# A fused attention, expert and slot-expert kernel on one core: a written-out sequence of all operations instead of priorities

## The chip, the core and the metric

The kernel runs on one NeuronCore of a Trainium2 chip. Its engines work in parallel, each through its own list of instructions, strictly in the order of the list: TensorE (PE, matrix products into the eight PSUM banks), VectorE (DVE), ScalarE (ACT), GpSimd (POOL) and SyncE (SP), which here issues all DMA transfers. They wait for each other by semaphores. The metric is the device time of one execution in microseconds (us); lower is better.

## What is computed

Three layers, on 4 x 576 = 2304 tokens of 512 features, all in float32:

```python
# 1: attention, 8 heads of 64, each token sees itself and the 63 tokens before it
scores = (q @ k.T) / 8, masked;  attn = softmax(scores);  x = attn @ v
# 2: a dense layer with mish
h = x @ w_in                      # 512 -> 2048
g = h * tanh(softplus(h))
y = g @ w_out                     # 2048 -> 512
# 3: soft routing to 8 experts of 4 slots
logits = y @ phi                  # 2304 x 32
d = softmax over tokens;  slot_input = d.T @ y
slot_out[e] = relu(slot_input[e] @ w1[e]) @ w2[e]
c = softmax over slots;   out = c @ slot_out
```

## The kernel before

The tokens form 18 tiles t of 128. The layer-2 output y is never formed: w_out is folded into phi (`wpmm`, from w_out transposed, tiles `wt`), so that logits come from g directly, and the sum over tokens is kept as A = d.T @ g (`A`, `Aup`) and multiplied by w_out (`wo`) once, in the tail.

Per attention tile, by the names of the operations: `qk` (scores, PE), `max`, `neg` (DVE), `exp` (ACT, two halves h of four heads), `sum`, `rcp` (DVE), `nrm` (POOL or DVE), `atr` (transposes of a half, PE), `tre` (their copy out of PSUM), `pv` (PE), `x` (copy). `vg` measures the size of a v tile for scaling. Then, per tile t and quarter m of w_in: `xh`, `xl` (x in two float16 parts), `mm{t}_{m}a` and `mm{t}_{m}b` (half products of six 128x512 float16 matmuls, line 727; the first two tiles use float32 in quarters 0 and 1, line 724), `mi` (mish, ACT, line 733), `gh`, `gl` (g in two float16 parts, lines 747 to 754), `tr` (a DMA transpose of both, issued by SP, line 760; tile 17 is transposed by PE instead), `lg` (logits), and per block of two tiles the running softmax over tokens `lt`, `bm`, `bexp`, `et`, `eh`, `el`, `A`, `Aup`. The weights w_in (`wi`), w_out (`wo`) and its transpose (`wt`) are loaded as 64-bit words and decoded to float32 by `a` (ACT, line 385), `b` and `d` (DVE, lines 390, 394). `wh`, `wl` are w_in in two float16 parts.

The tail: `tat`, `tate`, `tsi`, `tsie`, `tso`, `tsoe` (slot inputs), `t1` (16 products with w1), `relu`, `tho`, `thT`, `t2` (32 products with w2, line 1085, by column pieces of `W2C`), and for each piece `se`, `sr`, `sv` (spread the slot outputs), `fo` (products with c, line 1125), `ob` (copy, line 1131) and `st` (store, line 1138). w1 and w2 come as 64 loads `w0` to `w63` of 512 KB; each takes one of 53 slabs of SBUF, as do all k, q, v, weight and work tiles, and frees it after its last use.

ACT holds one table of functions at a time: exp and the decode use one (`E`), mish another (`M`); an `ACT_TABLE_LOAD` stands at each change. Copies and sums work with either.

The order is made when the program is built. `Plan` collects some 1,430 operations, each with an engine, a guessed cost, a priority, the operations it depends on and the buffers it takes and frees. `emit` then plays them through: whenever an engine is free in this play, it takes the ready operation of the lowest priority number whose buffers are free. The priorities are formulas of the tile number plus some 400 fitted shifts (`SHIFT`). `reserve` holds back slabs from the `w` loads. While PE would wait before the first quarter-3 product (`mm0_3a`), and again between the last product of tile 17 and `t1_0`, `emit` puts in pad products (`fill`, line 295: 128x256, of zeros, their result unused). What the program then contains is only the order on each engine; the costs play no part on the chip.

## Time and profile before

| | |
|---|---|
| runs (median of 3) | 388.83 us (387.75 to 388.90) |
| profiled execution | 387.64 us |
| its span | 385.8 us |
| PE busy | 368.3 us (95%) |
| DVE busy | 271.6 us (70%) |
| ACT busy | 255.0 us (66%) |
| POOL busy | 35.1 us (9%) |
| read from and written to HBM | 79.48 and 4.72 MB |
| instructions | 10397 |

The span is the time from the first to the last recorded work of the profiled execution. Busy is the union of an engine's instructions; a pad product counts as busy. The ends of matmuls are modelled, and in a row of back-to-back products the starts tell the pace. Idle time of an engine that is followed by other work is put down to what released it.

### The profile page before, as it was taken

To read this page: it belongs to the slowest core of one execution; us is meant where nothing else is said; L and a number is where in the kernel's file an instruction comes from. 1 tells how busy PE (TensorE), PEld (TensorE's weight loads), DVE (VectorE), ACT (ScalarE), POOL (GpSimd) and SP (SyncE) were. 2 spreads that over 40 slices of the span, in tenths; PEclk is the share of its full clock that TensorE was granted. 3 is DMA by queue.
4 is the path that set the end of the run, shared out by engine and by line. 5 is a ranking of instruction groups with operands and counts; after the bars stand their busy time and mean duration, and the time that the engine had idled before them with its cause. 6 is when DMAs were issued, how large, how long until landed. Compare 5 with 4: busy or idle time off the path is not lost.

```text
span 385.8 us, 10397 instructions
## 1 busy us (share of the span) xinstructions
PE 368.3 (95%) x4188; PEld 213.2 (55%) x4188; DVE 271.6 (70%) x781; ACT 255.0 (66%) x507; POOL 35.1 (9%) x33
## 2 busy tenths in 40 slices
PE   8999999999999798999999999999999999999981
PEld 6775646566655354685545445444644567534771
DVE  1879897798999878999999983678336567410241
ACT  2889999999999879799348744775299246000121
POOL 0033002605516000000000000000000000000000
PEclk9999999999999999999999999999999999999996
DMA  7999991079878989889899998999684999999996
GB/s 278 409 409 407 395 410 73 1 220 287 322 164 233 358 195 210 314 285 303 234 241 210 253 185 158 292 258 189 127 313 115 188 245 372 379 382 408 363 322 143
DMA packets 102912, 102.70 MB, mean 266 GB/s; under 512 B 78544, under 2 KB 83536, under 8 KB 102864
## 3 DMA queue, kind: packets, MB, share of 16 engines
q1 hardware_dynamic: 102864, 102.04, 89.7%
q8 instruction: 33, 0.54, 0.6%
q14 instruction: 15, 0.12, 0.1%
HBM read 79.48 MB, written 4.72 MB: 218 GB/s over the span
## 4 chain that ended last, share of the span: by engine, by line
PE 70%; DMA 10%; ACT 8%; DVE 6%; issue 3%; SPq 1%; DVEq 0%; ACTq 0%
PE h L727 32%; PE pad L295 4%; PE s L441 4%; PE eo L1085 4%; PE eh L1053 4%; DMA v<-in_vL 3%; PE px L526 3%; ACT p L469 3%; PE pt L513 3%; PE A L922 3%; DMA wor<-in_w_out 2%; PE lg L845 2%; PE h L724 2%; PE fo L1125 2%; DMA cst<-in_cst 2%
## 5 line engine op out<-in xcount | busy, mean ns | idle before, releaser
L727 PE MATMUL h<-wh,xx 128*128 128x512 f16 x544 | 171.6, 379 | 0.7 <-ACT pts L518 0.7
L727 PEld LDWEIGHTS <-xx 128*128 128x128 f16 x816 | 77.0, 98 | 88.3 <-issue 4.8
L727 PE MATMUL h<-wl,xx 128*128 128x512 f16 x272 | 103.1, 379 | 0.0
L733 ACT ACTIVATE u<-h,sc 128x512 f32<-128x512 f32 x68 | 44.0, 689 | 29.3 <-PE h L727 27.4
L754 DVE SCALAR_TENSOR_TENSOR gg<-u,sc,gg 128x1024 f16<-128x1024 f32 (+1 forms) x38 | 47.1, 1245 | 0.4
L733 ACT ACT_TABLE_LOAD x28 | 35.9, 1283 | 2.6 <-DVE wo L390 1.8
L483 POOL TENSOR_TENSOR p<-p,st 128x512 f32<-128x512 f32 x24 | 29.1, 1234 | 82.2 <-DVE sc L357 25.1
L469 ACT ACTIVATE p<-p,st 128x128 f32<-128x128 f32 x112 | 35.4, 394 | 0.1
L751 DVE TENSOR_SCALAR gg<-u,sc 128x1024 f16<-128x1024 f32 (+1 forms) x34 | 24.8, 741 | 11.9 <-ACT u L733 5.3
L462 DVE CUSTOM_DVE_ANT_0 p<-s,cb 128x128 f32<-128x128 f32 x112 | 25.5, 283 | 2.5 <-PE s L441 2.4
L295 PE MATMUL pad<-wphi 128*64 128x256 f16 x170 | 25.4, 299 | 0.9 <-DVE wphi L307 0.9
L513 PE MATMUL pt<-cst,p 128*128 128x128 f32 x144 | 22.1, 278 | 2.1 <-DVE st L462 1.6
L518 ACT COPY pts<-pt 128x512 f32<-128x512 f32 x36 | 20.7, 582 | 4.5 <-PE pt L513 4.5
L526 PEld LDWEIGHTS px<-pts,v 128*64 128x64 f32 x576 | 18.4, 138 | 8.1 <-issue 3.1
L526 PE MATMUL px<-pts,v 128*64 128x64 f32 x576 | 20.7, 225 | 2.0 <-DMA v<-in_vL 2.0
L295 PEld LDWEIGHTS <-wphi 128*64 128x64 f16 x170 | 18.8, 120 | 4.7 <-issue 2.0
L475 DVE TENSOR_REDUCE st<-p 128x4 f32<-128x512 f32 x28 | 18.8, 673 | 3.2 <-ACT p L469 3.1
L385 ACT ACT_TABLE_LOAD x14 | 18.0, 1283 | 4.3 <-DVE wo L394 1.4
L513 PEld LDWEIGHTS pt<-cst,p 128*128 128x128 f32 x144 | 16.1, 140 | 7.0 <-issue 2.3
L441 PE MATMUL s<-k,q 64*64 64x128 f32 x576 | 19.6, 275 | 0.0
L441 PEld LDWEIGHTS s<-k,q 64*64 64x64 f32 x576 | 15.5, 133 | 4.6 <-issue 2.6
L1131 ACT COPY ob<-fo 128x512 f32<-128x512 f32 (+3 forms) x14 | 5.3, 440 | 19.3 <-PE fo L1125 19.3
(175 smaller groups left out, 523.7 us busy)
## 6 DMA issues: line engine op xcount, KB each, us to landing
w<-in_wL SPq DMA_DIRECT2D x64, 512.0 KB, 7.0
v<-in_vL SPq DMA_DIRECT2D x18, 512.0 KB, 6.9
wir<-in_w_in SPq DMA_DIRECT2D x16, 512.0 KB, 9.7
wtr<-in_w_outT SPq DMA_DIRECT2D x16, 512.0 KB, 6.6
wor<-in_w_out SPq DMA_DIRECT2D x16, 512.0 KB, 4.6
k<-in_kL SPq DMA_DIRECT2D x12, 512.0 KB, 7.3
q<-in_qL SPq DMA_DIRECT2D x9, 512.0 KB, 9.3
out<-ob SPq DMA_DIRECT2D x6, 512.0 KB, 4.9
```

The lines of the kernel that those rows point to most:

```text
L295: PE.matmul(pad, lhsT=hot, rhs=hot.unsqueeze(1).to_broadcast([128, 4, 64]), start=True, stop=True)
L441: PE.matmul(st_[t][h][64 * c:64 * c + 64, p], lhsT=qt[t // 2][r, t % 2, p, 64 * c:64 * c + 64], rhs=kt[g // 3][r, p, 64 * (g % 3):64 * (g ...
L462: DVE.tensor_tensor_reduce(out=pr[t][:, h, p], in0=st_[t][h][:, p], in1=cb[:, mask(t)], scale=-0.125, scalar=3e38, op0=ALU.add, op1=ALU.mi ...
L469: ACT.activation(pr[t][:, h, p], (st_[t][h] if t < P["MP"] else pr[t][:, h])[:, p], AF.Exp, scale=0.125 if t < P["MP"] else -1.0, bias=sta ...
L483: (POOL if P["ND"] <= t < P["NRM"] else DVE).tensor_tensor(pr[t][:, h], pr[t][:, h], r, ALU.mult)
L513: PE.transpose(q[:, p], pr[t][:, h, p], ident)
L518: ACT.copy(ptS[t][:, h], pt_[t, h])
L526: PE.matmul(x[64 * h:64 * h + 64, p, f], lhsT=vt[t][:, c, 64 * (2 * p + h):64 * (2 * p + h) + 64], rhs=ptS[t][:, h, p, f], start=True, sto ...
L727: PE.matmul(ph[t, m], lhsT=xh[t][:, l, kk], rhs=r[m][:, kk], start=(kk == 0 and i == 0), stop=(kk == 3 and i == 2))
L733: ACT.activation(ub[t, h][:, m % 2], ph[t, m], AF.Mish, scale=1.0 if (t, m) in P["F32"] else col(INVH + 4 * PART[t] + m))
L751: DVE.tensor_scalar(o, u, col(CP + PART[t]), None, ALU.mult)
L754: DVE.scalar_tensor_tensor(gg[t, h][:, 1, c:c + n], flat(ub[t, h], c, n), col(CP + PART[t]), gg[t, h][:, 0, c:c + n], ALU.mult, ALU.subtract,)
```

## The change

All operations, their dependencies and their buffers stay, apart from four things. First, `emit` no longer chooses: it goes through a list of 1,428 names, `ORDER`, and issues each operation on its engine in that order. The priorities, the shifts and `reserve` are gone. The costs remain only to set where pads stand and which free slab is taken. Second, the engine of single casts and copies can be chosen one by one (`ENG`, `pick`, `two_ways`), and whether the row sums of a half tile's `exp` are made by ACT as it goes or by DVE afterwards. Third, the first q slab is loaded in two halves (`q0`, `q0b`), and tiles 0 and 1 invert their row sums by halves. Fourth, `W2C` has the columns 256, 128, 128 instead of 256, 128, 64, 64.

```diff
-    22, 19, 13, 3, 1, 0, 18, 12, 7), WQ=408.421, WQ_SP=1.144, A0=-11.663, A1=10, AK=12, A2=15, LEAD=15.837,
...
-    WO=-9.123, WO_SP=1.355, NU=9, NGC=14, NSC=4, FAST=2, PET=17, SINGLE=16, RB=8, W2C=((0, 256), (256, 128),
-    (384, 64), (448, 64)), QUART=17, VGA=(1, 3), TP=15.286, BL=66.703, NRM=13, VP=(-27.15, -25.68, -0.06,
...
+    PB=(2, 4, 8), NU=9, NGC=14, NSC=4, NX=2, PET=17, QUART=17, SINGLE=16, RB=8, RH=2, MP=4, VGN=2, GRAM=2,
+    TOP=0.77, W2C=((0, 256), (256, 128), (384, 128)), F32=((0, 0), (1, 0), (0, 1), (1, 1)),
+    ENG=dict(sum='000000000000000011001100110011001100110011001100010000000100110011',
+    nrm='0000110011001100110000000100100000000100010011001100110011000000000001',
...
+ORDER = """
+hot room_q0 q0 cb k0 cst wild0 wild2 eye k1 qk0 wia0 q0b max0_0 wild1 max0_1 wia2 neg0_1 neg0_0 q1 wib0 exp0_0 wib2
...
+gl1_0 qk11 v9
+tre7_0 xl4 wta5 atr7_1 nrm8_1 wtld14 pv6 gh0_1 max11_0 mm4_0a exp9_1 max11_1 v8 invh2_0 wtb5 atr8_0 tre7_1 sum9_1
+atr8_1 tre8_0 wtd5 mm4_3a wta11 gh1_0 max10_0 tre8_1 exp11_0 mm4_2a max10_1 rcp9 mm4_2b nrm9_0 sum11_0 exp11_1 xh5 xl5
+pv8 wta8 wtb11 sum11_1 wtd11 pv7 x6 v12 vg8 nrm9_1 wtb8 mm4_3b mi4_2 wtld13 gh3_0 atr9_0 wtd8 wtld9 wpmm1 tre9_0 rcp11
...
+""".split()
...
-    def emit(self):
...
-            for eng in sorted(ready, key=lambda x: x == "POOL"):
...
-                    k = prio[i] + (PRM["TP"] if o[8] and table and o[8] != table else 0.0)
-                    if (best is None or k < best[0]) and self.fits(o):
-                        best = (k, i)
...
+    def emit(self, order):
...
+        for name in order:
+            eng, cost, fn, deps, get, rel, tab = self.ops[name]
+            t = busy[eng]
...
+            elif eng == "PE":
+                while any(x in self.done and y not in self.done for x, y in self.warm):
+                    k = 0.11 if "qk0" in self.done else 0.22
+                    if busy[eng] + k > t + 1e-9:
+                        break
+                    self.fill()
+                    busy[eng] += k
+            busy[eng] = t + cost
...
+        def two_ways(name, act, dve, first_act):
+            o = [{name: ("ACT", act)}, {name: ("DVE", dve)}]
+            return plan.pick(name, o if first_act else o[::-1])[name]
...
+        for n, x in enumerate(("q0", "q0b")):
+            op(x, "SP", 0.67, lambda n=n: ld_q(0, slice(512 * n, 512 * n + 512)), ["room_q0"])
...
-                    accum_out=(stat[t][:, 1, 4 * h + p:4 * h + p + 1] if t < P["SUMA"] else None),
+                    accum_out=(stat[t][:, 1, 4 * h + p:4 * h + p + 1] if engine(f"sum{t}_{h}") == "NONE" else None),
...
-        plan.latest([f"mm{t}_0a" for t in range(P["LT"], NT)], P["XE"])
-        plan.emit()
+        plan.emit(ORDER)
```

In numbers of instructions, from the two built programs: pad products 170 before, 96 now. Before the first scores stand 41 and 30 of them, from there to about 21 us of the old time 39 and 33, from there to the first quarter-3 product 35 and 3, between the last product of tile 17 and `tsi` 56 and 30. ACT has 57 table loads before and 37 now; 22 more half tiles are summed by ACT inside `exp` (88 pieces of 128x128), and DVE has 22 row sums fewer (28, now 6). Of 34 `gh` casts of 128x1024, DVE had 30 and POOL 4; now DVE has 8, ACT 12, POOL 14. Of `wh`, ACT had 7 and DVE 1, now 2 and 6; of `nrm`, POOL had 24 and DVE 12, now 21 and 15; six `tre` copies go from ACT to DVE. The tail's `fo` has 36 narrow matmuls less and one `se`, `sr`, `sv` step less. Of the 64 `w` loads, 28 stood ahead of the last product of tile 17 in the old sequence, 31 in the new one; ahead of the 36th half product 5 before, 9 now.

The start of SP's list (a name ends with its tile and a running number), before:

```order
L377 DMA wir0_93<-in_w_in 128x1024
L424 DMA q0_102<-in_qL 128x1024
L420 DMA k0_110<-in_kL 128x1024
L409 DMA cb_70<-in_masks 128x384
L411 DMA cst_69<-in_cst 128x128
L377 DMA wir1_124<-in_w_in 128x1024
L377 DMA wir2_135<-in_w_in 128x1024
L420 DMA k1_165<-in_kL 128x1024
L428 DMA v0_170<-in_vL 128x1024
```

and now:

```order
L375 DMA q0_83<-in_qL 128x512
L357 DMA cb_70<-in_masks 128x384
L368 DMA k0_86<-in_kL 128x1024
L359 DMA cst_69<-in_cst 128x128
L326 DMA wir0_89<-in_w_in 128x1024
L326 DMA wir2_91<-in_w_in 128x1024
L368 DMA k1_94<-in_kL 128x1024
L375 DMA q0_83<-in_qL 128x512
L326 DMA wir1_153<-in_w_in 128x1024
L375 DMA q1_160<-in_qL 128x1024
L326 DMA wir3_218<-in_w_in 128x1024
L379 DMA v0_228<-in_vL 128x1024
```

What the first scores need (q, k, masks, identity) stands ahead of the first w_in tile, with half of q; two more slabs stand ahead of v0.

SP's list where the transposes (`gT<-gg`, tile and half) meet the late v loads, before:

```order
L760 DMA_TRANSPOSE gT0_1_1614<-gg0_1_1411 128x16x128
L377 DMA wtr7_1665<-in_w_outT 128x1024
L760 DMA_TRANSPOSE gT1_1_1684<-gg1_1_1444 128x16x128
L428 DMA v9_1721<-in_vL 128x1024
L377 DMA wtr11_1744<-in_w_outT 128x1024
L377 DMA wtr2_1758<-in_w_outT 128x1024
L420 DMA k9_1769<-in_kL 128x1024
L377 DMA wtr1_1793<-in_w_outT 128x1024
L428 DMA v11_1811<-in_vL 128x1024
```

and now:

```order
L709 DMA_TRANSPOSE gT0_1_1740<-gg0_1_1447 128x16x128
L709 DMA_TRANSPOSE gT3_0_1787<-gg3_0_1592 128x16x128
L375 DMA q8_1816<-in_qL 128x1024
L379 DMA v10_1840<-in_vL 128x1024
L368 DMA k10_1854<-in_kL 128x1024
L326 DMA wor0_1864<-in_w_out 128x1024
L368 DMA k11_1878<-in_kL 128x1024
L379 DMA v11_1903<-in_vL 128x1024
L709 DMA_TRANSPOSE gT0_0_1922<-gg0_0_1785 128x16x128
L709 DMA_TRANSPOSE gT1_1_1975<-gg1_1_1702 128x16x128
L326 DMA wor4_2016<-in_w_out 128x1024
L379 DMA v14_2055<-in_vL 128x1024
```

Before, four transposes stand among the 16 loads of w_out transposed (`wtr`); now all 16, and v8, v9 and v12, stand ahead of the first transpose, and w_out loads (`wor`) stand among the transposes instead. Right behind what is shown come, now, a transpose, a slot load, v17 and v13.

## Rows read from the trace of the kernel before

**Rows 1.** Busy time by stage: us, then PE, PEld, DVE, ACT, POOL, clock, DMA share, GB/s

```profile
21.00:67.00 46.00, 45.23 (x440) 27.01 (x441) 39.66 (x133) 42.52 (x104) 8.40 (x7) 1.00 0.87 340
67.00:106.00 39.00, 39.00 (x445) 23.83 (x446) 34.88 (x142) 38.28 (x77) 16.83 (x14) 1.00 0.66 205
106.00:165.00 59.00, 53.44 (x593) 30.88 (x593) 51.41 (x179) 51.11 (x110) 7.80 (x6) 1.00 0.90 246
165.00:316.10 151.10, 150.58 (x1414) 78.71 (x1411) 112.45 (x228) 96.71 (x141) 0.74 (x1) 1.00 0.95 222
316.10:332.60 16.50, 16.50 (x227) 11.52 (x226) 12.26 (x42) 8.59 (x20) 0.00 (x0) 1.00 1.01 371
332.60:378.70 46.10, 43.69 (x873) 25.90 (x872) 9.86 (x29) 6.32 (x18) 0.00 (x0) 1.00 0.99 360
```

**Rows 2.** The same view for the pad products alone

```profile
21.00:67.00 46.00, 3.63 (x23) 1.00 0.87 340
67.00:106.00 39.00, 1.40 (x12) 1.00 0.66 205
316.10:332.60 16.50, 7.92 (x56) 1.00 1.01 371
```

**Rows 3.** Chain of waits, whole span: start us, us, what

```profile
10.39 2.52 PE pad L295 x22
...
122.83 7.69 DMA v<-in_vL
...
144.38 5.61 DMA v<-in_vL
...
162.92 1.30 PE h L727 x6
...
164.21 0.44 PE pt L513 x4
```

**Rows 4.** The page's 40 slices of the span: GB/s moved by DMA

```profile
GB/s 278 409 409 407 395 410 73 1 220 287 322 164 233 358 195 210 314 285 303 234 241 210 253 185 158 292 258 189 127 313 115 188 245 372 379 382 408 363 322 143
```

**Rows 5.** ACT by line (busy, mean ns) and in order of time (start us, us)

```profile
L733 ACT ACT_TABLE_LOAD x28 | 35.9, 1283 | 2.6 <-DVE wo L390 1.8 <-DVE gg L754 0.4
...
L589 ACT ACTIVATE wh<-wi,sc 128x1024 f16<-128x1024 f32 x7 | 8.2, 1165 | 0.0
...
23.51 0.37 ACT L469 ACTIVATE p<-s,st 128x128 f32<-128x128 f32 x1
...
23.86 0.38 ACT L469 ACTIVATE p<-s,st 128x128 f32<-128x128 f32 x1
...
82.43 1.27 ACT L469 ACTIVATE p<-p,st 128x128 f32<-128x128 f32 x4
```

**Rows 6.** DVE by line, whole span, last row 60 to 130 us, while POOL casts

```profile
L751 DVE TENSOR_SCALAR gg<-u,sc 128x1024 f16<-128x1024 f32 x30 | 22.8, 776 | 11.9 <-ACT u L733 5.3 <-PE lg L847 5.1 <-PE px L526 1.4
L475 DVE TENSOR_REDUCE st<-p 128x4 f32<-128x512 f32 x28 | 18.8, 673 | 3.2 <-ACT p L469 3.1
...
L751 DVE TENSOR_SCALAR gg<-u,sc 128x1024 f16<-128x1024 f32 x1 | 1.5, 1530 | 0.0
```

**Rows 7.** SP's queue in order of time, and a DMA group's median to landing

```profile
109.56 2.08 SPq L760 DMA_TRANSPOSE gT<-gg  x1
...
112.66 3.99 SPq L760 DMA_TRANSPOSE gT<-gg  x1
...
v<-in_vL SPq DMA_DIRECT2D x18, 512.0 KB, 6.9
```

**Rows 8.** The tail in order of time, and two groups of stores

```profile
364.12 1.96 PE L1085 MATMUL eo<-w,tw 128*32 128x128 f32 x80
...
367.51 1.99 PE L1085 MATMUL eo<-w,tw 128*32 128x64 f32 x128
...
out<-ob SPq DMA_DIRECT2D x6, 512.0 KB, 4.9
out<-ob SPq DMA_DIRECT2D x5, 256.0 KB, 3.3
```

More of the change, by code (lines that the diff above doesn't have):

```diff
@@ L94 @@
+ob0_2_1 ob0_2_2 st1_2_0 st0_2_0 ob0_2_3 st0_2_1
+""".split()
 class Plan:
@@ L126, in op, with pick @@
+    def pick(self, var, options):
+        f, i, rest = re.match(r"([A-Za-z]+)(\d*)(.*)", var).groups()
+        i = int(i or 0) * 4 + int(rest[1:] or 0)
+        s = PRM["ENG"].get(f, "")
+        self.choices[var] = (f, i, options)
+        return options[int(s[i]) if i < len(s) else 0]
+    def op(self, name, eng, cost, fn, deps=(), get=(), rel=(), table=None):
+        assert name not in self.ops, name
+        self.ops[name] = (eng, cost, fn, list(deps), list(get), list(rel), table)
         for k in rel:
@@ new lines, in emit @@
+    def emit(self, order):
+        assert sorted(order) == sorted(self.ops), sorted(set(order) ^ set(self.ops))
+        end, freed = {}, Counter()
+        busy = Counter(SP=self.BOOT)
+        table, turned, port, held = None, False, 0.0, 0.0
+        self.order = []
+        for name in order:
+            eng, cost, fn, deps, get, rel, tab = self.ops[name]
+            t = busy[eng]
+            for d in deps:
+                e = self.ops[d][0]
+                t = max(t, end[d] + (self.SAME[e] if e == eng else self.PIPE[e] + self.INTO[eng]))
+            for key, p in get:
+                f, i = heapq.heappop(self.free[p])
+                t = max(t, f)
+                self.where[key] = (p, i)
+            if tab and tab != table:
+                table = tab
+                cost += self.SWITCH
+            if eng == "SP":
+                cost += self.TURN * (turned and not name.startswith("tr"))
+                turned = name.startswith("tr")
+            elif eng == "POOL":
+                t = max(t, held)
+                port = t + cost
+            elif eng == "DVE" and name.startswith(self.PORT):
+                cost += max(0.0, port - t)
+                held = t + cost
+            elif eng == "PE":
[6 more added lines that the diff above has]
+            busy[eng] = t + cost
+            end[name] = t + cost + (self.DMA if eng == "SP" else 0.0)
+            fn()
+            self.done.add(name)
+            self.order.append((t, end[name], eng, name))
+            for key in rel:
+                freed[key] = max(freed[key], end[name] + 0.2)
+                self.refs[key] -= 1
+                if not self.refs[key]:
+                    p, i = self.where[key]
+                    heapq.heappush(self.free[p], (freed[key], i))
@@ L561, in body @@
                 if mp:
-                    op(f"neg{t}_{h}", "DVE", 0.07, e + 1.5, lambda t=t, h=h: t_neg(t, h), [f"max{t}_{h}"])
-                op(f"exp{t}_{h}", "ACT", (1.37 if t < P["SUMA"] else 1.0) + 0.17 * (not mp), e + 2, lambda t=t, h=h: t_exp(t, h), [f"neg{t}_{h}" if mp else f"max{t}_{h}"] + ([f"exp{t}_0"] if h else []), rel=free if mp else [], table="E")
-                if t >= P["SUMA"]:
-                    op(f"sum{t}_{h}", "DVE", 0.6, e + 3, lambda t=t, h=h: t_sum(t, h), [f"exp{t}_{h}"] + (["sum%d_0" % t] if h else []))
@@ L572, in body @@
-            op(f"pv{t}", "PE", 1.1, k + 9, lambda t=t: t_pv(t), [f"tre{t}_0", f"tre{t}_1", f"v{t}"], get=[(f"px{t}", "b")],
+                    op(f"neg{t}_{h}", "DVE", 0.07, lambda t=t, h=h: t_neg(t, h), [f"max{t}_{h}"])
+                x, s_ = f"exp{t}_{h}", f"sum{t}_{h}"
+                o = [{x: ("ACT", 1.0 + 0.17 * (not mp)), s_: ("DVE", 0.6)}, {x: ("ACT", 1.37 + 0.17 * (not mp)), s_: ("NONE", 0.0)}]
+                o = plan.pick(s_, o[::-1] if t < 4 else o)
+                op(x, *o[x], lambda t=t, h=h: t_exp(t, h), [f"neg{t}_{h}" if mp else f"max{t}_{h}"] + ([f"exp{t}_0"] if h else []), rel=free if mp else [], table="E")
```

600 lines of the change are left out of this document (239 added, 361 removed), and 4 rows, old and new, of the table WO.

## The prediction, made before the changed kernel ran

> **What bounds the kernel now.** I read the busy time by stage first [rows 1]. The stages are: start up to 21 us (not shown), attention with the first expert products up to 165, expert products up to 316.1, a turn of 16.5 us in which the last blocks of the soft-routing are folded in, the slot experts up to 378.7, and 7.1 us of last copies and stores up to 385.8. The reader is to see that TensorE (PE) has work nearly always: from 165 to 316.1 it is busy 150.58 of 151.1 us, so nothing can be won there by order alone. It lacks work in three places. From 106 to 165 it is busy 53.44 of 59 us, 5.6 us idle. In 21 to 106 and in the turn the busy time hides idleness, since the kernel fills its waits with pad products that compute nothing; these stand in the second view [rows 2]: 23 + 12 pads, and 56 in the turn. The chain of waits gives a pad's real price, 22 in 2.52 us or 0.115 us each [rows 3], and names what PE waited for from 106 to 165: two loads of v tiles, 7.69 and 5.61 us on the chain [rows 3]. ScalarE (ACT) is the partner in the early stages: 42.52 of 46 and 38.28 of 39 us [rows 1].
>
> So what an order can win lies in about 0.8 + 4.0 us (21 to 106: idle, and 35 pads), 5.6 us (106 to 165), 56 x 0.115 = 6.4 us (turn), and in start and end. The sum is made against the profiled execution, 387.64 us; its span is 385.8, and 1.8 us lie around it. The median of the runs shown is 388.83, 1.2 us more.
>
> **The change part by part.**
>
> *First query slab in halves, and in front.* Ahead of the first scores the queue had 512 + 512 + 512 + 96 + 64 = 1,696 KB, now 256 + 96 + 512 + 64 = 928 KB. The 768 KB less are 0.786 MB; at the 409 GB/s of the second of the page's 40 slices [rows 4] that is 1.9 us. Against this, v0 now has 4.4 MB ahead of it instead of 3.3 (two slabs more): 2.6 us later at the same rate, if the first weighted sum of values feels it, and the gain is gone. The one issue more lies under transfers that keep the DMA full. Bounds: 0 and -1.9. I take **-1.9**, because the new listing puts no more pads after the first scores than the old one up to the same place (33 against 39), so it sees no new wait there.
>
> *Pads from 21 to 106.* The new listing has 3 pads where the old one has 35: 32 x 0.115 = 3.7 us, with the 0.8 us idle 4.5. It can hold only if ACT and VectorE (DVE) deliver earlier. ACT: 20 table loads fewer at 1.283 us are -25.7 us; 22 half tiles of exp now also sum their rows, and the accumulating pieces start 0.35 us apart, 1.4 us for four, where four plain ones take 1.27 [rows 5], so at most 0.2 us per half tile, +4.4; 12 gh casts come to ACT, with no row of their own, at the 1.165 us of the nearest cast (wh) +14.0; five wh casts leave, -5.8. In all -13 us, though most of the table loads fall away only after 165. DVE: 22 row sums at 0.673 and 22 gh casts at 0.776 leave, -31.9; 14 copies, casts and normalisations come, about 0.7 us each by the same rows, +9.8; in all -22 us [rows 6]. Bounds: 0 and -4.5; I would take -3.5.
> One row speaks against it: GpSimd (POOL) gets 14 gh casts instead of 4, and in the stretch where POOL casts, DVE's own cast of that form took 1530 ns instead of 776 [rows 6]. Ten such hits less the three normalisations that leave POOL are 7 x 0.75 = 5.3 us of DVE, a quarter of what it gains, spread over a longer stretch than this. I take off 0.5: **-3.0**. The Trainium skill, GPSIMD Engine Reference, section Key points, says that GpSimd shares its SBUF interfaces with VectorE and contends with VectorE's two-port and two-input instructions; read as exclusion for the whole of all 10 casts it would cost 10 x 1.53 = 15 us of the 22, this term would be -1.2 and the sum below 378.5. The trace agrees with the rule in that one cast, which took twice its time, not in that extent.
>
> *106 to 165, the v loads.* All loads stand on one queue, SP's, and a transpose there waits for its gl tile. The two transposes of 109.56 and 112.66 held it until 116.65, with a single load between [rows 7]; the v load at 122.83 came late by that, and the one at 144.38 stood right behind another. In the new list all 16 loads of w_out transposed and v8, v9, v12 stand ahead of the first transpose; v10 stands behind three transposes with one load between them, v14 behind two more, v13 behind another. A v load takes 6.9 us to land in the median [rows 7]. What covers it is the matrix work that the list puts between load and use. For v8 that is two transposed halves at 0.44 and three half products at 1.30 [rows 3], 4.8 us: 2.1 short. Counted in the same way v11 has 6.3 (0.6 short), v10 8.7, v13 9.2, v14 10.8. So 2.7 of the 5.6 us stay: **-2.9**. Bounds: -5.6, and the other way the slower case below.
>
> *165 to 316.1.* PE is full and does the same products: **0**. The cover is the product work itself; if it went, ACT (96.71 of 151.1 us busy, less the table loads) is next.
>
> *The turn.* 30 pads stand between the last expert product and the first slot product instead of 56: 26 x 0.115 = 3.0. The products, folds and copies of the chain are the same, and the column sums of the second softmax group now stand behind the fold on DVE. Bounds: 0 and -4 (some idle between the pads). I take **-2.7**.
>
> *w2 by 256, 128, 128.* 256 matmul rows of 64 columns at 1.99/128 = 0.0155 us become 128 of 128 columns at 1.96/80 = 0.0245 [rows 8]: -0.8. One expand step and 36 output products of the narrow form go: no row of theirs stands here; at the price of a wide w2 row they are -0.9, at three times it -2.7, and I take -1.8. But the last piece is twice as wide: its stores are 512 instead of 256 KB, 4.9 instead of 3.3 us to landing [rows 8], +1.6, and two copies more per engine, about +0.6 at the 0.67 us of a 512-wide DVE pass less what the narrow ones took. In all -0.8 - 1.8 + 1.6 + 0.6 = **-0.4**; bounds -3.5 (the wider end hidden) and +2.2 (nothing gained).
>
> **Sum:** -1.9 - 3.0 - 2.9 - 2.7 - 0.4 = -10.9, and 387.64 - 10.9 = **376.7 us**, 12.1 below the median of the runs.
>
> **The rivals.**
>
> *The slot weights become the bound.* From 106 on DMA is 0.90 to 1.01 busy [rows 1]. If PE is earlier but the weight stream isn't, the tail waits. By the new list 31 of 64 slot loads stand ahead of the last expert product, 28 before: 3 x 0.524 MB at 360 GB/s are 4.4 us of stream, and 1.9 come from the start: 387.6 - 6.3 = 381.3 us. For it: DMA is 0.99 busy in the tail. Against it: 0.34 x 39 us of DMA are idle in 67 to 106 [rows 1], and the new list has nine slot loads issued by the 36th half product, the old one five. Chance 0.21.
>
> *Slower: late v tiles.* One mechanism, at the queue of SP between 106 and 165: if a gl tile isn't ready when its transpose comes up, the loads behind stand. With two transposes costing 7.1 us as above, v10 is 7.1 + 6.9 - 8.7 = 5.3 short, v14 3.2, v13 behind a single one of 4.0 us 1.7 (4.0 + 6.9 - 9.2), with v11 and v8 12.9 in all instead of 5.6; the pads then come back too, since the early decodes wait for the same queue. 387.6 - 1.9 - 2.7 - 0.4 + 7.3 = 389.9 us. It decides from the point where the second of two neighbouring transposes waits for DVE. For it: just that happened twice before; against it: DVE has 22 us less to do. Chance 0.12.
>
> *Nothing moves:* each gain is taken up by the next wait, about 387. Chance 0.06.
>
> *The clock.* With fewer pads PE could be idle enough to lose its 2.4 GHz. In the trace the granted clock is 1.00 in every stage up to 378.7, also in 106 to 165 with 5.6 us idle and no pad [rows 1]. If the turn (16.5 us, of which 6.4 are pads, so some 9 us of work) ran at 1.2 GHz, it would cost up to 9: 385.9. Chance 0.03. The Trainium skill, TensorE: Matmul & The Clock Gate, section on the HAM clock gate, says that the array falls to half rate when it has been idle for a while. By that rule fewer pads could bring the case just priced; the trace does not show it before 378.7.
>
> **How the numbers follow.** The forecast has 0.58. The three ways that end faster have 0.58 + 0.21 + 0.03 = 0.82, no change 0.06, slower 0.12; 0.3%, about 1.2 us, is what a measurement of this kernel can tell from no change. The low end takes all favourable bounds: 387.6 - 1.9 - 4.5 - 5.6 - 4.0 - 3.5 = 368.1, so 368; the high end takes in the bound by the weight stream and the clock case, 386, and leaves out no change and slower, 0.18.
>
> **What would show it.** In the profile after: first scores some 1.9 us earlier; hardly a pad between the third tile's scores and the turn; ACT with 37 table loads; PE idle below 3 us in 106 to 165, with v8 rather than two later tiles as the one that ends a wait; about 30 pads in the turn; last store 512 KB. Wrong would be: PE idle above 5 us behind v10, v13 or v14; a chain that names slot weights in the tail; a clock below 1.00 before 370; or PE with new idleness in 165 to 316, where this reckoning sees none.

## The result, and the profile after

| | before | changed |
|---|---|---|
| median of 4 runs | 388.29 us (387.64 to 388.90) | 371.45 us (370.91 to 373.18) |
| ratio, 95% interval | | 0.957 (0.954 to 0.961) |
| profiled execution, its span | 387.64, 385.8 us | 373.18, 371.4 us |

The change makes the kernel 4.3% faster. That is 5.2 us more than was forecast, inside the range given. The profiled execution of the changed kernel is the slowest of its four; a second profile of the same program stands among the experiments.

The engines' busy time and the table loads, from the page of the changed kernel:

```profile
PE 357.4 (96%) x3948; PEld 204.1 (55%) x3948; DVE 252.8 (68%) x750; ACT 240.8 (65%) x573; POOL 45.8 (12%) x40
...
L681 ACT ACT_TABLE_LOAD x18 | 23.1, 1283 | 1.9 <-DVE gg L703 1.1
```

DVE is 18.8 us less busy than before, ACT 14.2 less, POOL 10.7 more. The table loads on all lines of ACT are 37, as the order had told; before there were 57.

Busy time by stage, with the stages' ends moved to where the same work ends now (columns as in [rows 1]: us, PE, PEld, DVE, ACT, POOL, clock, DMA share, GB/s):

```profile
21.00:67.00 46.00, 46.00 (x461) 27.00 (x460) 43.99 (x171) 45.05 (x140) 7.85 (x8) 1.00 1.03 407
67.00:106.00 39.00, 38.95 (x419) 22.70 (x421) 36.06 (x134) 37.60 (x102) 6.49 (x5) 1.00 0.75 256
106.00:165.00 59.00, 56.71 (x721) 34.00 (x714) 52.18 (x176) 53.25 (x143) 20.63 (x14) 0.97 1.08 242
165.00:308.20 143.20, 142.55 (x1233) 73.05 (x1230) 89.52 (x179) 80.42 (x119) 9.32 (x8) 1.00 0.89 211
308.20:320.70 12.50, 12.50 (x189) 8.61 (x189) 10.12 (x36) 5.94 (x14) 0.74 (x1) 1.00 0.97 340
320.70:363.60 42.90, 42.34 (x709) 24.31 (x708) 9.79 (x27) 6.21 (x16) 0.00 (x0) 1.00 1.02 387
```

The same view for the pad products alone (us, PE busy and count, clock, DMA share, GB/s):

```profile
0.00:21.00 21.00, 9.83 (x66) 1.00 0.89 327
21.00:67.00 46.00, 0.00 (x0) 1.00 1.03 407
67.00:106.00 39.00, 0.00 (x0) 1.00 0.75 256
308.20:320.70 12.50, 4.36 (x30) 1.00 0.97 340
```

Against [rows 1, 2]: the 35 pads between 21 and 106 us are gone, with the idle time beside them, and the turn has 30 pads instead of 56. The last expert product ends at 308.2 us instead of 316.1 (-7.9), the turn lasts 12.5 us instead of 16.5 (-4.0), the stretch from there to the last output product 42.9 instead of 46.1 (-3.2), and what follows it 7.8 instead of 7.1 (+0.7). That is the 14.4 us between the two spans.

What the changed kernel still waits for stands in its chain of waits (start us, us, what):

```profile
4.05 8.85 DMA q<-in_qL
...
144.72 8.89 DMA gT<-gg
...
217.70 6.33 DMA gT<-gg
```

No v load is left in it. A transpose took that place. The length of a piece of the chain is not the time that PE stood: the load or transpose runs beside other work, and PE stands only at its end. For the transpose of 8.89 us PE stood 2.29 us, at the first logits product of block 1, as its timeline shows (start us, us, line, operation, in brackets the idle time and what ended it):

```profile
150.98 0.38 PE L675 MATMUL h<-wh,xx 128*128 128x512 f16 x1
153.65 0.41 PE L790 MATMUL lg<-wphi,gT 128*128 128x64 f16 x8 [2.29 <-DMA gT<-gg]
```

Behind that wait the granted clock fell, by windows of 2 us (us, PE busy, clock, DMA share, GB/s):

```profile
152.00:154.00 2.00, 0.35 (x12) 1.00 1.26 287
154.00:156.00 2.00, 2.00 (x17) 0.66 1.21 182
156.00:158.00 2.00, 2.00 (x33) 0.50 0.81 277
158.00:160.00 2.00, 2.00 (x15) 0.99 0.75 247
```

0.50 is the lower level, 1.2 GHz. Against full speed the two windows lost 2 x 0.34 + 2 x 0.50 = 1.7 us, so wait and slow clock took 4.0 us at this place, in this execution. What taking them away is worth is a question for the experiments.

### The profile page after: what moved, and what is told of

Same layout as the page of the kernel before. It is cut to its first block, busy times and chain, and to the rows that moved or that the text cites. A ratio compares the mean times of both kernels' runs of the same rounds, so it can differ in the third digit from the quotient of the medians.

```text
span 371.4 us, 9932 instructions
## 1 busy us (share of the span) xinstructions
PE 357.4 (96%) x3948; PEld 204.1 (55%) x3948; DVE 252.8 (68%) x750; ACT 240.8 (65%) x573; POOL 45.8 (12%) x40
## 4 chain that ended last, share of the span: by engine, by line
PE 87%; DMA 6%; SPq 2%; DVE 1%; ACT 0%; issue 0%; ACTq 0%
PE h L675 44%; PE px L478 5%; PE pt L465 5%; PE s L392 4%; DMA gT<-gg 4%; PE eo L1023 4%; PE h L672 4%; PE eh L991 4%; PE A L867 3%; DMA q<-in_qL 2%; PE lg L790 2%; PE lg L792 2%; SPq L709 1%; PE pad L245 1%; PE fo L1063 1%; PE wpo L613 1%
## 5 line engine op out<-in xcount | busy, mean ns | idle before, releaser
L703 DVE SCALAR_TENSOR_TENSOR gg<-u,sc,gg 128x1024 f16<-128x1024 f32 (+1 forms) x38 | 48.1, 1276 | 15.1 <-ACT gg L698 12.2
L420 ACT ACTIVATE p<-p,st 128x128 f32<-128x128 f32 x112 | 41.5, 393 | 0.0
L435 POOL TENSOR_TENSOR p<-p,st 128x512 f32<-128x512 f32 x21 | 26.8, 1289 | 94.3 <-DVE st L431 47.8
L696 POOL TENSOR_SCALAR gg<-u,sc 128x1024 f16<-128x1024 f32 x14 | 18.2, 1301 | 154.4 <-ACT u L681 72.1
L470 ACT COPY pts<-pt 128x512 f32<-128x512 f32 x30 | 17.2, 581 | 1.8 <-PE pt L465 1.7
L334 ACT ACTIVATE woy<-wor 128x512 f32<-128x512 f32 x16 | 10.3, 667 | 11.3 <-DMA wor<-in_w_out 8.2
L1069 ACT COPY ob<-fo 128x512 f32<-128x512 f32 (+1 forms) x10 | 5.2, 570 | 18.4 <-PE fo L1063 18.4
L420 ACT ACTIVATION_READ_ACCUMULATOR p<-p,st 128x1 f32 x88 | 17.0, 193 | 0.0
L790 PE MATMUL lg<-wphi,gT 128*128 128x64 f16 x288 | 14.3, 193 | 2.5 <-DMA gT<-gg 2.5
```

The source lines that it names most:

```text
L334: ACT.activation(y[j // 2][:, j % 2], raw[j][:, :, 1].bitcast(F32), AF.Prelu, scale=2.0 ** -112, alpha=2.0 ** 32)
L420: ACT.activation(pr[t][:, h, p], (st_[t][h] if t < P["MP"] else pr[t][:, h])[:, p], AF.Exp, scale=0.125 if t < P["MP"] else -1.0, bias=sta ...
L435: ENG[engine(f"nrm{t}_{h}")].tensor_tensor(pr[t][:, h], pr[t][:, h], r, ALU.mult)
L696: POOL.tensor_scalar(o, u, col(CP + PART[t]), 1.0, ALU.mult, ALU.mult)
L703: DVE.scalar_tensor_tensor(gg[t, h][:, 1, c:c + n], flat(ub[t, h], c, n), col(CP + PART[t]), gg[t, h][:, 0, c:c + n], ALU.mult, ALU.subtract,)
L790: PE.matmul(lg[b][:, j], lhsT=gT[t, h][:, 0, k], rhs=wphi[:, 8 * h + k], start=(h == 0 and k == 0), stop=False)
```

## The experiments

Two questions were open. Which part of the change carries the gain before 316 us, the order or the engines? And why did the tail give 3.2 us where a fraction was expected? The runs came in three groups, each on a chip of its own, with its own runs of the kernel before (medians 389.79, 388.74 and 388.58 us); ratios are to those. The first group has the runs of 382.8, 383.0, 370.98 and 370.24 us, the second those of 372.37, 394.69, 370.17 and 377.85, the third the other four. The changed kernel ran beside the second group only, so runs of the others are compared with it by ratio, which is 0.957 for the changed kernel both times.

### Order and engines, a square of four

The first corner has the new order with the old engines, all but those of the tail's last copies:

```diff
-    ENG=dict(sum='000000000000000011001100110011001100110011001100010000000100110011',
-    nrm='0000110011001100110000000100100000000100010011001100110011000000000001',
-    tre='000000000000000000000000100001000000000000000000010000001100000001',
-    x='000010000000000010000000000000000000000000001000000000001', wh='00001000100000001000100010001',
-    gh='22002000120002001100220011000200210020002200020011000100010011002',
-    vghT='00000000000000000000000000000000000000000000000000000000000000000000011',
-    vglT='000000000000000000000000000000000000000000000000000000000000000000001', tsie='1', tsoe='10001',
-    thT='100000000000000000000000000000000000000010001', ob='01101000000100010000100001'),
+    ENG=dict(nrm='00001100110011001100110011001100110011001100110011', wh='00000000000000000000000000001', gh='220022', thT='100000000000000000000000000000000000000010001', ob='01101000000100010000100001'),
```

> The new list of operations with the engines of before: every row sum from the third part of the tiles on goes back to DVE, tiles 1 to 12 normalize half on POOL again, the gh casts, decodes and small copies go where they were. Theory A (engines and order each pay for their own part: the engines hold the 3.0 us of idle and pads from 21 to 106 us, the order the rest): 371.5 + 3.0 = 374.5 us, with 6 to 7 us more DVE work than in the changed kernel before 106 us and some 20 pads there. Theory B (the list was made for its engines, so an operation that comes late on DVE holds all that stands behind it in the fixed order): 380 us or more, with new idle time of PE after 106 us as well. Theory C (engines do nothing, all is the order): 371.5 us.

Measured: 382.8 us, ratio 0.983 (0.979 to 0.987): theory B. The second corner has the old order up to the first product of the slot weights, as a list, with the old engines and the new tail:

```diff
 ORDER = """
-hot room_q0 q0 cb k0 cst wild0 wild2 eye k1 qk0 wia0 q0b max0_0 wild1 max0_1 wia2 neg0_1 neg0_0 q1 wib0 exp0_0 wib2
...
+hot ones wild0 room_q0 q0 q0b k0 wia0 cb cst wild1 wib0 wild2 wid0 eye idh qk0 k1 wia1 v0 max0_0 wib1 wia2 neg0_0 max0_1
...
```

> The order and the engines of before, written as a list, up to the first product of the slot weights; what is left of the change is the first query slab in halves, the reciprocals of tiles 0 and 1 by halves, and the new tail with the w2 columns of 256, 128, 128. By the prediction's terms: 388.3 - 1.9 (front) - 0.4 (columns) = 386.0 us. By the trace of the changed kernel, where the stretch from the first si product to the last output product is 3.5 us shorter and the end behind it 1.0 longer: 388.3 - 1.1 - 2.5 = 384.7 us if the shorter tail belongs to the columns; then the stretch of eo products is some 2 us shorter here too. Third theory (the tail is short only because the order ahead of it loaded more weights earlier, and halves of a slab bring nothing): 388.3 us.

Measured: 383.0 us, 0.983 (0.979 to 0.987), some 6 us below before and lower than all three theories. Of the 5.9 us between the two profiled spans, 2.9 lie behind the last expert product, in the tail. The other 3.0 lie ahead of it, where both programs have nearly the same operations in the same order: in 106 to 165 us PE was idle for 3.17 us here and for 5.56 before. Whether that comes from the small changes at the front or only from the execution is not shown. It warns against taking the waits of one profile for those of the program.

The third corner has the same list as the second, with the engines of the change left as they are:

> The order of before up to the first product of the slot weights with the engines of the change, and the new tail: the fourth corner of the square with the order and the engines, after 371.5 (new, new), 382.8 (new order, old engines) and 383.0 (old, old). If the two parts add up, 383.0 - (382.8 - 371.5) = 371.7 us: the engines alone bring all but the tail. If each needs the other, 383 us or more: the operations moved to ACT and POOL then come too late for an order that was found for DVE, with waits for exp pieces and POOL products of a microsecond or two and pads between 21 and 106 us as before.

Measured: 394.69 us, 1.014 (1.010 to 1.019), slower than before.

So from the corner that is old in both, the new order alone brings nothing (383.0 to 382.8), the new engines alone cost about 12 us (11.7 by the medians), and both together bring about 11. Theories that give each its own share are out. The pages suggest why. ACT's groups with table loads in the third corner, columns: busy us, mean ns, idle before:

```profile
L680 ACT ACT_TABLE_LOAD x28 | 35.9, 1283 | 5.1 <-PE A L866 3.5 <-DVE wo L338 1.2
...
L419 ACT ACTIVATION_READ_ACCUMULATOR p<-p,st 128x1 f32 x88 | 16.7, 190 | 0.0
```

and the busy time of the corners, old order with new engines, then new order with old engines:

```profile
PE 369.2 (95%) x4039; PEld 211.6 (54%) x4039; DVE 254.5 (65%) x750; ACT 267.9 (69%) x593; POOL 43.5 (11%) x40
```

```profile
PE 364.0 (96%) x3999; PEld 209.1 (55%) x3999; DVE 268.9 (71%) x782; ACT 228.2 (60%) x482; POOL 36.3 (10%) x33
```

The order decides the table loads: 57 in both corners with the old one, 37 in both with the new one, a difference of 20 x 1.283 = 25.7 us of ACT. The engines decide who sums the rows: on ACT's accumulation they cost ACT 16.7 us, on DVE 14.8. The new order with the old engines leaves ACT with 228 us of work and DVE as loaded as ever; the old order with the new engines puts the sums on an ACT that still has its 57 table loads, and PE there waits for ACT's copies and expert units (1.75, 1.55, 0.78 and 1.12 us at 105, 128, 181 and 211 us). Read so, only both together spend on the sums what the order saved. That it is the table loads, and not another property of the order, is argued from these pages: no run puts the loads back into the new order.

One more run takes back the sums alone:

```diff
-    ENG=dict(sum='000000000000000011001100110011001100110011001100010000000100110011',
-    nrm='0000110011001100110000000100100000000100010011001100110011000000000001',
+    ENG=dict(nrm='0000110011001100110000000100100000000100010011001100110011000000000001',
...
```

> The changed kernel with the 22 row sums that ACT's accumulation does since the change back on DVE (22 x 0.673 = 14.8 us more DVE work, 22 x 0.77 = 17 us less on ACT), order and other engines as changed. Theory A (a sum costs what it holds up in the order it stands in; of the 11.3 us that the old engines cost in the new order, the sums hold the larger part): 377 to 380 us, with pads back between 40 and 80 us and PE idle between 100 and 170 us. Theory B (the sums are hidden beside the matrix work as long as DVE has slack; casts and normalization on POOL make the difference): 372.5 us. The prediction's term for the whole of the engines before 106 us, 3.0 us: 375.4 us.

Measured: 379.03 us, 0.976 (0.972 to 0.980), some 7 us above the changed kernel by ratio: theory A. Its pads and two of its waits on PE:

```profile
21.00:67.00 46.00, 2.83 (x19) 1.00 1.03 407
67.00:106.00 39.00, 1.69 (x12) 1.00 0.66 227
```

```profile
119.07 0.39 PE L668 MATMUL h<-wh,xx 128*128 128x512 f16 x1 [1.17 <-DVE st L406]
...
134.40 0.63 PE L458 MATMUL pt<-cst,p 128*128 128x128 f32 x4 [1.83 <-DVE p L428]
```

31 pads are back before 106 us, and PE waits for DVE's maxima and normalizing behind it. The last expert product ends at 313.4 us, 8.2 later than in the second profile of the changed kernel. Of the 10 to 11 us that the old engines cost in the new order, the sums hold some 7; the other engines were not tried one by one.

### The v loads of the old order

Three loads moved in the second corner's list: v11 and v13 change places, and v14 goes ahead of a transpose (one operation a line; `vg11` and `vg13`, which follow the first two on ACT, change places with them):

```diff
 tre7_0
-v13
+v11
 sum11_0
...
 xh6
-v11
+v13
 wta2
...
 exp14_0
+v14
 tr2_0
...
 exp13_0
-v14
 mm7_2a
```

> The old order with the old engines and the new tail, as the run of 383.0 us, with two loads moved on SP's queue: v11 takes the place of v13 (17.4 us earlier, and v13 its place), v14 goes ahead of the transpose that it stood behind. Theory of the prediction (PE stands for late v tiles in 106 to 165 us): the wait of 1.47 us for v at 129.35 us and its slow start go, 1.5 to 2.9 us less: 380.1 to 381.5 us. Rival 1 (PE's order then waits for the next thing, the copies and decodes in 120 to 150 us): 382.5 to 383 us. Rival 2 (v13, now later, or the transpose behind v14 is waited for instead): 383 us or more.

Measured: 384.25 us, 0.989 (0.985 to 0.993), where the corner itself had 0.983: no gain, if anything a loss of 2 us, with intervals that barely overlap. The corner had 1.47 us of waiting for v; that is gone, and PE's idle time in 106 to 165 us is 3.49 us instead of 3.17. Two of the waits that PE shows instead:

```profile
131.61 0.38 PE L667 MATMUL h<-wh,xx 128*128 128x512 f16 x1 [0.72 <-ACT u L673]
147.62 0.66 PE L457 MATMUL pt<-cst,p 128*128 128x128 f32 x4 [1.65 <-DVE st L405]
```

DVE's maximum is late by 1.65 us at 147.6, where the corner had 0.70 us of idle time at the same product. So in the old order the late v tile was the wait that ended last, with ACT and DVE close behind it; taking it away gives nothing. The waits are those of rival 1 (ACT and DVE, no v load and no wait for v13), the time is above its range; where the rest of the loss lies is not shown.

### The query slab in halves

```diff
-        for n, x in enumerate(("q0", "q0b")):
-            op(x, "SP", 0.67, lambda n=n: ld_q(0, slice(512 * n, 512 * n + 512)), ["room_q0"])
+        op("q0", "SP", 1.33, lambda: ld_q(0, slice(0, 1024)), ["room_q0"])
+        op("q0b", "NONE", 0.0, lambda: None, ["q0"])
```

> The changed kernel with the first query slab loaded by one DMA of 512 KB again, all else as in the changed kernel. Theory of the prediction (first scores 1.9 us earlier by the half slab): 371.5 + 1.9 = 373.4 us, first scores at about the time of before. Theory of the trace (only 1.1 us of work was gained in the first 20 us, and the second scores wait for the second half): 371.5 + 1.1 = 372.6 us or less. Rival (the loads of the front are a stream that feeds PE only as fast as it comes, so the order within it is worth nothing after the second tile): 371.5 us.

Measured: 370.98 us, 0.953 (0.950 to 0.957), no slower than the changed kernel. The first scores start at 7.58 us; with the halves they started at 7.25 and 6.83 us in the two profiles of the changed kernel. The second scores start at 11.99 us, with the halves at 12.94, behind a wait of 0.55 us for q, and at 11.90 without one. So the halves' worth is lost in what executions differ by. In the old order they bring nothing either: the second corner has its first scores at 8.94 us and the third tile's at 19.42, before had 8.75 and 19.34. The new order with the whole slab has the third tile's at 15.53. The front's gain is the order's.

### The wait for the transpose

A second profile of the changed kernel, unaltered:

> The changed kernel as it is, for the chip on which the next ones run; its profile is a second one of the same program. All theories: 370.9 to 373.2 us as before. If the wait of 2.29 us for a transpose at 153.65 us and the granted clock of 0.83 behind it belong to the program, they stand here again; if they belong to the one profiled execution (373.18 us, the slowest of four), they are shorter here, and the time is near 371.0.

Measured: 372.37 us, 0.957 (0.954 to 0.960); the profiled execution had 369.83 us, the fastest of six. The wait stands there again, shorter, and the clock of the next windows stays up:

```profile
152.11 0.41 PE L790 MATMUL lg<-wphi,gT 128*128 128x64 f16 x8 [1.49 <-DMA gT<-gg]
```

```profile
152.00:154.00 2.00, 1.89 (x24) 1.00 1.02 217
154.00:156.00 2.00, 2.00 (x38) 1.00 0.90 305
```

The wait belongs to the program; its length is the execution's (2.29, 1.49, and 0.94 to 2.16 us in the four other programs with the new order and engines up to there that keep the product in its place). With 2.29 us the clock fell, in the other five it stayed up. Between the two profiles of the changed kernel, 2.4 of the 3.4 us of difference arise at this place and most of the rest ahead of 22 us, where PE waits for the first slabs. Moved out of the way:

```diff
 wpil0
-lg1_0_0
 v15
 exp17_0
 lr0
 mm7_0a
...
 mm7_0b
+lg1_0_0
 sum16_0
```

> The changed kernel with one operation moved: the first logits product of block 1, at which PE stood 2.29 us for a transpose of tile 2, comes after the product mm7_0b instead of ahead of mm7_0a. Theory: PE does the products of tile 7 and the attention product of tile 13 in the time of the wait; the idle of 2.3 us and the slow matmuls behind it (granted clock 0.83 in the ten microseconds, some 1.6 us) are gone: 371.5 - 3.9 = 367.6 us. Rival 1 (products of tile 7 were not ready either, the wait goes to another product): 371 to 371.5 us. Rival 2 (the gain is made, then given back in the tail, where the weights stream at 407 GB/s and PE waits for it): 370 to 371 us, with the last product of tile 17 some 3.9 us earlier and PE idle in the tail.

Measured: 370.24 us, 0.950 (0.947 to 0.954). The 367.6 us of the theory did not come. PE has no wait for a transpose there, and 0.5 us of one at a later place; but its last expert product ends at 305.6 us, where the two profiles of the changed kernel have 308.2 and 305.2. The theory had taken the wait of one execution, the longest of those profiled, for the wait of the program. With the slab whole as well:

> The changed kernel with the first logits product of block 1 behind mm7_0b and the first query slab loaded whole. Theory (the logits move takes 2 to 4 us of stall and slow clock away, the half slab is worth nothing): equal to the run with the logits alone, so 0.950 of before and 0.5 to 1 per cent below the changed kernel on the same chip. Rival 1 (both only shift when the transposes run, the stall moves on): equal to the changed kernel. Rival 2 (halves are worth their 1.1 us when nothing else is in the way): 1 us above the run with the logits alone.

Measured: 370.17 us, 0.953 (0.950 to 0.956), 2.2 us below the changed kernel on the same chip, highest run 371.67 against 373.53. Windows of the two stretches around the place, all engines (PE first):

```profile
150.00:160.00 10.00, 10.00 (x131) 5.84 (x130) 8.35 (x31) 8.51 (x29) 1.93 (x2) 1.00 1.15 214
160.00:170.00 10.00, 9.05 (x68) 5.08 (x67) 6.56 (x19) 8.86 (x17) 0.43 (x1) 1.00 0.71 155
```

150 to 160 is full now, and 0.95 us of idle time has moved to the next ten. The two versions have the lowest medians of this study. The intervals of their ratios overlap with the changed kernel's (0.954 to 0.960), or touch it, so a gain of 0.4 to 0.7% is likely and not shown beyond that.

### The tail

The tail of before, its columns and the old order of the tail's operations, behind the changed kernel:

```diff
-    TOP=0.77, W2C=((0, 256), (256, 128), (384, 128)), F32=((0, 0), (1, 0), (0, 1), (1, 1)),
+    TOP=0.77, W2C=((0, 256), (256, 128), (384, 64), (448, 64)), F32=((0, 0), (1, 0), (0, 1), (1, 1)),
```

> The changed kernel up to the first product of the slot weights, then the tail of before: w2 columns of 256, 128, 64, 64 with the operations of the tail in the order of before. The prediction's term: + 0.4 us (128 eo products of 64 columns instead of 64 of 128). The term as the trace of the old order with the new tail has it (si to last output product 43.0 us instead of 46.3, the end behind it 0.8 longer): + 2.5 us, of which 0.5 is in the eo products and 2.4 in two gaps of PE in the last rounds of eo and output products (1.0 and 1.4 us in before). Rival (the weights stream sets the tail, the columns cost nothing): 0.

Measured: 377.85 us, 0.972 (0.969 to 0.975), 5.5 us above the changed kernel on the same chip, more than any of the expectations. In the traces the stretch from the last expert product to the end takes 67.4 us, against 63.2 and 62.9 in the two profiles of the changed kernel: 4.2 to 4.5 us of it. Its chain of waits, the last rounds of eo products (the slot experts' second products, `t2`) and output products:

```profile
355.76 1.90 PE eo L1023 x122
357.66 1.96 issue
...
361.24 1.36 PE eo L1023 x86
362.60 0.74 issue
```

The same rounds in the changed kernel:

```profile
356.29 1.10 PE fo L1063 x32
357.39 2.99 PE eo L1023 x96
360.38 0.90 PE fo L1063 x8
```

With columns of 64, PE stands for 2.7 us at nothing that the profile names ("issue"); before had such gaps of 1.01 and 1.38 us in the same place. With columns of 128 most programs have none; two have one, shorter: 0.49 us in the first corner, and 0.80 us in the run that takes back the sums:

```profile
364.81 1.28 PE L1016 MATMUL eo<-w,tw 128*32 128x128 f32 x34 [0.80 <-issue]
```

Two runs part the columns' costs. Stores alone in rows of 256 bytes:

```diff
-            SP.dma_start(o, ob[b, c, h].rearrange("p n i d -> p (n i) d"))
+            x = ob[b, c, h].rearrange("p n i d -> p (n i) d")
+            for z in (slice(0, 64), slice(64, 128)) if c == 2 else (slice(0, d),):
+                SP.dma_start(o[:, :, z], x[:, :, z])
```

> The changed kernel with the three output stores of the last 128 columns each as two DMAs of 64 columns, so in rows of 256 bytes; products and copies as in the changed kernel. Theory P (what the columns of 64 cost is the short rows: under them the queue moved 147 GB/s at a share of 0.73 in the last 5 us of before, 148 at 0.54 in the last 3 us of the changed kernel, so 201 and 274 GB/s at full share, and the 1.18 MB of the last 128 columns take 5.9 us instead of 4.3): + 1.6 us, 374.0 us. Rival (the cost lies in the products, the copies and PE's gaps ahead of them): within 0.3 per cent of the changed kernel, 372.4 us.

Measured: 373.12 us, 0.961 (0.958 to 0.965). That is 0.75 us above the changed kernel's 372.37 by the medians of two chips, and 1.6 us by the ratios, whose intervals overlap. The traces decide: from the last output product to the end this run takes 9.5 us, the changed kernel 7.9 and 8.0 in its two profiles, 1.4 to 1.6 us less. Window after the last products, of this run and of the second profile of the changed kernel (last two columns: DMA share and GB/s):

```profile
365.00:370.00 5.00, 0.00 (x0) 0.00 (x0) 0.00 (x0) 0.00 (x0) 0.00 (x0) 0.50 1.04 211
```

```profile
360.00:365.00 5.00, 0.01 (x1) 0.00 (x0) 1.09 (x3) 1.35 (x3) 0.00 (x0) 0.90 0.93 264
```

Short rows move 203 GB/s at full share where rows of 512 bytes move 284. So theory P holds, in direction and size. The Trainium skill, DMA: Bandwidth & Descriptors, section on why small descriptors are slow, names a fixed overhead for each packet, 27% for a descriptor of 256 bytes. These two windows agree in direction; their 28% less is a rough figure, since the stores don't fill them evenly, and not a test of the 27%, since by the same page rows of 512 bytes bear the overhead too.

Products alone in columns of 64:

```diff
-                    PE.matmul(
-                        tl["o", c][32 * j:32 * j + 32], lhsT=tl["hT"][:, i, kf + k].rearrange("p j s -> p (j s)"), rhs=v[:, j, k],
...
+                    r = slice(32 * j, 32 * j + 32)
+                    outs = [(tl["o", c][r, 0:64], v[:, j, k, 0:64]), (tl["x", c][r], v[:, j, k, 64:128])] if c == 2 else [(tl["o", c][r], v[:, j, k])]
+                    for o, y in outs:
+                        PE.matmul(
+                            o, lhsT=tl["hT"][:, i, kf + k].rearrange("p j s -> p (j s)"), rhs=y,
...
```

> The changed kernel with each eo product of the last 128 columns written as two of 64 columns into two banks, and one copy more to gather them: 64 products and weight loads more on PE, loads and stores as in the changed kernel. Products alone: 128 x 0.0158 instead of 64 x 0.0236 us, + 0.5 us, 372.9 us. Theory I (the gaps of 1.96 and 0.74 us that PE shows ahead of eo products of 64 columns, with nothing that it waits for, come from PE's own stream of instructions, which is longer by those products): + 0.5 to + 2.7 us, with such gaps in its trace between 350 us and the last output product. If the gaps don't show, they belong to the stores or the order of the old tail.

Measured: 379.67 us, 0.976 (0.971 to 0.980), 7.2 us above the changed kernel by ratio, with its loads and stores as they were; the expectation had at most 2.7. In the traces the stretch from the last expert product to the end is longer by 4.5 to 4.8 us; the front, which the edit leaves alone, came 2.1 to 3.2 us later than in the two profiles of the changed kernel, so not all of the 7.2 is the products'. The expectation counted calls; each leaves two records in the trace, so the products alone are 256 x 0.0155 - 128 x 0.0245 = +0.8 us. Most of the rest is this, in its chain:

```profile
358.63 1.05 issue
...
361.73 2.78 issue
```

The groups of the eo products (busy us, mean ns, idle before) name 3.8 us of it, and the output products behind the gaps are slower, with a granted clock of 0.57 from 366 to 370 us:

```profile
L1027 PE MATMUL eo<-w,tw 128*32 128x64 f32 x128 | 4.4, 223 | 3.9 <-issue 3.8
L1071 PE MATMUL fo<-os,A 32*128 32x128 f32 x64 | 3.2, 356 | 0.4 <-DVE os L1049 0.4
```

The last pair took 2.07 us where the changed kernel took 1.18. So the gaps come with the number of products, without any change to a load, a store or the slot weights (one copy and one PSUM bank more came with them).

That PE's own instructions come too late there is a reading that the traces support. Of the DMA queue that the profile calls "instruction" (q8 on the page), every program has one packet of 16 KB for some 260 of PE's products and weight loads together: 33 packets before, 31 now. Five programs show eight gaps of this kind (before, this run and the old tail two each, the first corner and the run with the sums on DVE one each), and each of the eight ends 1.2 to 1.5 us after such a packet has landed. Waits for DVE in the same stretch, of 0.4 to 0.5 us, end 0.8 to 4.7 us behind a packet. At 0.0155 us a product [rows 8] 64 columns also use up a packet's instructions faster than 128 columns do at 0.0245. No run varied the supply itself, so this stays a correlation; what is shown by experiment is that more and smaller products bring longer gaps.

## Why the prediction was right, and where its terms were off

The direction, the place of most of the gain and the signs of it were as said; the sum was short by 14.4 - 10.9 = 3.5 us of span. That it came so near is partly luck: the step for 106 to 165 us promised too much for a wrong reason, and three others too little. Term by term:

- **The front, -1.9.** Measured by what is left of the 7.9 us when the next two terms are taken off: -7.9 + 4.8 + 1.6 = -1.5, and 66 pads before 21 us instead of 80, which is 14 x 0.115 = 1.6 us. Size right, reason wrong. First scores came at 7.25 instead of 8.75 us as said, but with the slab in one piece the kernel is no slower, and halves in the old order bring nothing. The front gained by the order of the list, which brought the third tile's scores to 15.35 us from 19.34. A front with the halves is itself uncertain by some 3 us: five programs that are the same up to there have the first expert product between 19.82 and 22.97 us.
- **Pads from 21 to 106, -3.0.** 35 pads at the chain's pace of 2.52/22 = 0.115 us, with 0.77 us of idle time beside them [rows 1 to 3], are 4.8 us; 0.05 us of idle time is left. Direction right, undersized by 1.8. The step took work off ACT and DVE as two sums that each count. The square shows that they are one thing: the order makes room on ACT, the engines fill it, and neither half alone brings a microsecond. The 0.5 us taken off for casts on POOL had no ground. In the kernel before, DVE's one long cast (91.75 to 93.28 us) ran beside two normalizations on POOL, not beside a cast; now, with 14 casts on POOL, none of DVE's eight took long:

```profile
L700 DVE TENSOR_SCALAR gg<-u,sc 128x1024 f16<-128x1024 f32 x8 | 6.0, 749 | 0.7 <-issue 0.7
```


- **The v loads, -2.9.** The step that failed. It took the two v loads on the chain, 7.69 and 5.61 us long, for what PE waited for, and so put all of PE's 5.56 us of idle time down to them. The timeline of the kernel before shows what PE did stand for, and ACT at the second load:

```profile
127.19 0.38 PE L727 MATMUL h<-wh,xx 128*128 128x512 f16 x1 [0.70 <-ACT pts L518]
...
130.65 1.15 PE L526 MATMUL px<-pts,v 128*64 128x64 f32 x32 [2.01 <-DMA v<-in_vL]
...
148.96 0.66 PE L513 MATMUL pt<-cst,p 128*128 128x128 f32 x4 [1.56 <-DVE st L462]
...
158.66 0.66 PE L679 MATMUL wpt<-cst,wps 128*128 128x128 f32 x4 [0.76 <-DVE wps L671]
```

```profile
150.07 0.60 ACT L496 ACTIVATE vj<-v 128x512 f32<-128x512 f32 x1 [0.58 <-DMA v<-in_vL]
```

Only 2.01 of the 5.56 us are a v load. At the second load ACT stood, for 0.58 us, and by the chain PE felt it at most in the 0.76 us behind DVE; the rest is DVE's maxima and ACT's copies. In the changed kernel all of these waits are gone, and one that the prediction had not named, the first logits product behind its transpose, came with 2.29 us, and the slower clock behind it with 1.7: 5.56 - 2.29 - 1.7 = 1.6 us gained. That moving v loads is not what gained them shows in the old order, where it took PE's v wait away and brought nothing. PE's idle time stayed under 3 us there as said, but not behind v8.
- **165 to 316, 0.** 0.52 us of idle time before, 0.65 now: right.
- **The turn, -2.7.** 30 pads as said, and 12.5 us instead of 16.5: -4.0. The 26 pads less are 3.0 us; the further microsecond is less time between the pads, which no run takes apart.
- **The w2 columns, -0.4.** The term that was mis-sized most beside the v loads: 42.9 instead of 46.1 us up to the last output product and 0.7 more behind it make -2.5. The old order with the new tail has 43.0 us from the first si product (`tsi`) to the last output product, against 46.3 before, and the changed kernel with the old tail is 5.5 us slower in all. The step set +1.6 for wider stores and +0.6 for copies against the gain. In place of those the runs show that narrow stores cost time themselves (1.4 to 1.6 us for the last 128 columns), that the end behind the last product is only 0.7 us longer, and that PE's nameless gaps (2.4 us in the chain of before, at 371 and 376 us) come with more and narrower products. The step had no term for such gaps, though they stood in the trace of before.

Of the rivals, the bound by the slot weights didn't come: no weight load stands in the chain of the tail. The clock did fall, as a sign that was listed against the forecast, but for 4 us at 154 to 158 and not in the turn. The late v tiles of the slower rival didn't come either; its place, SP's queue with two transposes in a row, was the right one, and what came late there was the transpose itself.

## What to carry to other kernels

An order and a choice of engines are one decision: sums moved to an engine pay only if the order has freed that engine first, so test them together, and read the count of table loads before moving work to ACT. A long load in the chain of waits is not time that the engine stood: read the idle time before each of its instructions in the timeline. And a wait is worth its length only if what stands behind it is early, and if it stands there in a second profile too; look at both before pricing it. At the end of a kernel, where nothing covers PE, fewer and wider products can be worth several times their own time.

## What was not expected of the hardware

- PE's gaps with nothing to wait for, 0.7 to 2.8 us long, two in the last 25 us of each of the three programs with eo products of 64 columns (before, the old tail behind the new order, the products split). Of the ten programs with 128 columns two have one, of 0.49 and 0.80 us. All eight end 1.2 to 1.5 us after a packet of the "instruction" queue.
- The wait for the same transpose differed from 1.49 to 2.29 us between two executions of one program; 2.29 us of idle PE was followed by 4 us at a granted clock of 0.66 and 0.50, 1.49 us by 1.00. So 0.8 us more of waiting went with 2.5 us more of time at that place.
